# A hand-written list of 1026 operations, put in another order: linear attention and an MLP mixer on one core

## The chip, the core and the metric

The kernel runs on one core of a Trainium2 chip. The core has TensorE (PE in the profile; its weight loads are PEld), VectorE (DVE), ScalarE (ACT), GpSimd (POOL) and SyncE (SP), each with its own queue of instructions that it works off in order. DMAs are issued by SP, ACT and POOL and carried by 16 DMA engines. Matmul results land in PSUM, which the kernel cuts into eight banks of 128 x 512 fp32. The metric is the device time of one execution in microseconds; the time of a kernel is the median of its runs.

## What is computed

Inputs are q, k, v and f_logit (4 batches, 8 heads, 768 steps, 48 channels per head) and four weight matrices. Attention is a recurrence over the steps with a forget gate, and its output, as x of 768 x 384 per batch, goes through a mixer over tokens and one over channels:

```python
f = 1.0 / (1.0 + np.exp(-f_logit))
for t in range(S):
    state = f[:, :, t, :, None] * state + np.einsum('bhd,bhe->bhde', k[:, :, t], v[:, :, t])
    y[:, :, t] = np.einsum('bhd,bhde->bhe', q[:, :, t], state)
...
h = np.maximum(xt @ w_tok1, 0.0) @ w_tok2
u = x + h.transpose(0, 2, 1)
h2 = np.maximum(u @ w_ch1, 0.0) @ w_ch2
return (u + h2).astype(np.float32)
```

## The kernel before

**Attention, per batch b (0 to 3) and chunk P (0 to 2), 256 steps each.** The loads bring f, k, q and v of a chunk (POOL's DMAs, cast to bf16 for k, q, v; the first f loads go by SP and ACT). ScalarE makes the gate's logarithm: Exp and Ln at L457 and L459, or Softplus at L454 for the first two chunks. VectorE adds pairs of steps (`two`, L448; for later batches also the remainder `two_lo`, L470), PE sums them over the steps by a triangular matrix (`sums`, L479 to L482, and `totals`, L486), VectorE forms `first` (L499), ScalarE takes four exponentials (`GG`, L502 and L519) and the decay of a block (`glast`, L505, or `ends`, L509, with a small DMA on SP, L515). VectorE multiplies q and k by them (`qk`, L448, two instructions a chunk).

q and k are then transposed. Batches 0 and 1 do it on PE (L546) with a copy out of PSUM to qT and kT (L434 on ScalarE, L436 on VectorE). Batches 2 and 3 (`TURNED = 2`) do it by DMA transposes on SP (L531, "turned tiles"): kT directly, qT by way of qJ and a copy on POOL or ScalarE (L438, L434). Then come on PE the scores (L581), the parts of the state (L599), and, when VectorE (L624), or for four tiles ScalarE and POOL (L619, L621), has masked the scores to `AmT`, the outputs (L665) with the carried state (L657). VectorE carries `state` on (L633 to L641), and copies to `state_bd` follow on POOL, ACT or DVE.

**Mixer, per batch.** Outputs are copied to `x_bf` and `x_nat`; tok1 (L709, twelve matmuls), `h1T`, tok2 (L725), `u_bf`; a transpose to `uT`, on PE (L766) for batches 0 and 1 and by DMA on SP (L755, `U_TURNED`) for batches 2 and 3; ch1 (L784, 24 groups of three matmuls of 384 columns) with a ReLU to `zT` on ScalarE or VectorE (L443, L445); ch2 (L803, groups of four matmuls); the addition to `x_nat` (L814) and the store on SP (L702).

**What sets the order.** The body of the kernel issues nothing but a few memsets: `add` notes each operation with the engines that may do it, what it needs and makes, its PSUM bank and a kind for its cost. `Plan.best` then walks the constant `ORDER`. A code c stands for operation c // 4, on its engine number c % 4:

```python
for code in ORDER:
    op = self.ops[code // 4]
    e = op.engine = op.engines[code % 4]
```

For each it works out a start from what the operation needs, from its engine and its bank, takes the bank that comes free first, puts idle matmuls (`steady`, L852) into longer pauses of PE ahead of 25.5 us of its own count, and sorts by start; the operations are issued in that order. Thus the order on each engine's queue is that of `ORDER`, and the planner's times settle the banks and the number of idle matmuls. The constants `HELD` and `SLOTS` say when it takes the first loads to land, and it lets POOL hold eight loads under way.

Of the kernel before, what the change touches and what calls it, by code (L numbers as in the profile page):

```python
# [20 lines left out]
TURNED = 2  # L21
NQ = 2
ORDER = (
    0, 4, 12, 16, 24, 28, 32, 8, 20, 188, 192, 196, 36, 40, 44, 76, 68, 48, 52, 60, 208, 356, 212, 220, 64, 224,
    236, 240, 228, 360, 364, 368, 248, 244, 216, 376, 232, 372, 380, 388, 260, 80, 84, 265, 384, 200, 88, 296,
    252, 92, 96, 56, 300, 256, 72, 309, 304, 396, 392, 204, 312, 268, 272, 504, 408, 400, 276, 288, 404, 316,
    292, 280, 413, 508, 512, 320, 324, 100, 104, 108, 416, 420, 516, 448, 428, 452, 536, 532, 524, 520, 461,
    457, 544, 540, 112, 116, 120, 284, 124, 128, 132, 432, 136, 328, 332, 340, 440, 344, 464, 336, 468, 348,
    352, 444, 140, 476, 472, 556, 561, 528, 436, 424, 548, 552, 704, 592, 676, 708, 680, 564, 568, 596, 576,
    572, 584, 588, 580, 480, 484, 488, 600, 604, 608, 612, 616, 493, 497, 144, 148, 152, 501, 621, 624, 156,  # L30
    712, 684, 688, 692, 696, 716, 720, 724, 700, 728, 780, 812, 732, 736, 784, 816, 796, 800, 748, 752, 764,
    768, 820, 804, 740, 789, 756, 772, 808, 792, 852, 860, 868, 865, 856, 872, 844, 836, 828, 1188, 1192, 849,
    833, 972, 976, 824, 744, 776, 840, 1212, 1216, 980, 1036, 1012, 1028, 948, 1033, 760, 1220, 1224, 953, 1040,
    984, 1016, 996, 1020, 1001, 1025, 1004, 932, 1009, 1044, 988, 1060, 892, 1236, 1232, 1244, 1228, 1248, 1064,
    1048, 896, 1196, 1200, 1252, 1256, 993, 937, 1268, 1273, 1260, 900, 916, 1052, 876, 884, 905, 1264, 920,
    1056, 880, 888, 1368, 1372, 1276, 1280, 1284, 1288, 1292, 1240, 160, 164, 168, 172, 1376, 176, 180, 184,
    628, 1300, 1304, 1312, 1388, 1392, 1384, 1316, 1204, 1320, 1128, 908, 1132, 924, 1308, 1296, 1324, 1408,
    1380, 913, 1168, 1340, 1344, 1136, 940, 964, 1348, 1208, 1528, 1328, 1532, 1400, 1404, 928, 1336, 1356, 968,
    1352, 944, 1412, 1140, 1536, 1540, 1424, 1564, 1560, 1544, 1548, 1552, 1416, 1172, 1176, 956, 1108, 1429,
    1420, 1180, 960, 1572, 1568, 1432, 1436, 1440, 1444, 1448, 632, 636, 640, 644, 2204, 1332, 1364, 1360, 1396,  # L40
    1556, 1184, 1456, 1464, 1468, 1452, 1472, 1112, 1584, 1576, 1580, 1088, 1092, 1484, 1460, 2208, 1588, 2212,
    1480, 1476, 2216, 1592, 1596, 1600, 1604, 1096, 1612, 1608, 1500, 1504, 1488, 1620, 1624, 1616, 1496, 1492,
    1512, 1628, 1068, 1508, 1744, 1716, 1720, 1724, 1748, 1516, 1520, 1636, 1632, 1524, 2228, 2232, 2388, 1640,
    1644, 1752, 1648, 1728, 2236, 1116, 1652, 1656, 1660, 1664, 1732, 1736, 1756, 2392, 2240, 2264, 2260, 2244,
    2248, 648, 652, 656, 660, 664, 668, 672, 1668, 1120, 1760, 1741, 1764, 1769, 1072, 2396, 2272, 2268, 1808,
    1820, 1832, 1812, 1148, 1784, 1836, 2252, 2412, 2408, 1816, 1840, 1824, 1828, 2404, 1796, 1772, 1152, 1788,
    1800, 1776, 2284, 1884, 1868, 1876, 1888, 1880, 1872, 2276, 1076, 3144, 1780, 1792, 1804, 2400, 1156, 2044,
    2004, 2220, 2420, 2424, 1080, 1160, 1100, 2009, 2432, 2428, 1860, 2068, 2076, 2280, 1844, 2028, 1864, 2293,
    2072, 1996, 1848, 2001, 2012, 1852, 2036, 2224, 2048, 2016, 1856, 2552, 2288, 2020, 2025, 2556, 2040, 2080,
    2032, 1988, 1916, 1992, 2296, 2300, 2304, 2308, 2312, 1920, 3148, 1672, 2416, 1084, 2256, 2444, 2436, 1676,  # L50
    2316, 2332, 2560, 2564, 1932, 2340, 1936, 1964, 1956, 2052, 2324, 2328, 2057, 2320, 1968, 2336, 2576, 2572,
    2568, 2440, 2060, 1908, 2588, 1912, 2584, 3168, 2344, 1961, 3172, 2348, 2596, 2184, 1892, 1900, 2448, 1896,
    2064, 1904, 2188, 1680, 2452, 1684, 1688, 1692, 2456, 2460, 2464, 2468, 2472, 2476, 2592, 2144, 3176, 2148,
    2192, 2488, 2480, 2492, 2360, 2364, 2368, 2580, 2608, 2600, 3180, 2352, 2356, 2496, 1696, 1700, 2505, 2196,
    3184, 3200, 3204, 2484, 2381, 3212, 3188, 3192, 2376, 3208, 1980, 2152, 2164, 2168, 2384, 3152, 2373, 1704,
    2501, 2508, 1985, 2512, 2521, 2517, 2617, 1924, 1940, 1945, 2604, 2172, 2176, 2524, 2528, 2532, 2612, 2156,
    1708, 1712, 1928, 2540, 3156, 2548, 2544, 2536, 3160, 2620, 2624, 2628, 2632, 2636, 2648, 2652, 2640, 2644,
    2656, 2104, 2665, 2660, 3164, 3328, 3332, 1948, 2724, 2728, 2084, 3492, 1953, 2732, 2696, 2700, 2668, 2672,
    2676, 2704, 2736, 2680, 2685, 2688, 1972, 2708, 2712, 2740, 2716, 2744, 2088, 3336, 2721, 1977, 3496, 3196,
    3224, 3216, 2748, 2752, 2756, 2764, 3220, 2776, 2768, 2780, 2092, 2800, 2804, 3352, 3348, 2692, 2784, 3340,  # L60
    2808, 3344, 3360, 2761, 2773, 3232, 3228, 2788, 2812, 2108, 2124, 2112, 2816, 2096, 2792, 2821, 3368, 2796,
    3364, 3236, 3240, 3244, 3248, 3252, 3260, 2128, 3500, 2132, 2824, 2828, 3372, 3272, 3268, 3264, 2848, 2856,
    2860, 2852, 2136, 3256, 3504, 2116, 2888, 2864, 2880, 2832, 3528, 3512, 3284, 3000, 2984, 3276, 3280, 2892,
    2837, 2989, 3300, 3304, 3317, 3005, 3524, 2868, 3508, 3516, 2884, 2976, 2960, 2840, 2928, 3532, 2980, 2933,
    2944, 2968, 2936, 2949, 3016, 2844, 2964, 3536, 3288, 3384, 2973, 2941, 2872, 2920, 3380, 2896, 2952, 2957,
    2876, 3020, 3313, 2924, 2900, 2912, 2916, 2904, 2909, 3308, 3388, 3044, 3376, 1104, 3520, 1124, 3356, 3548,
    1144, 3540, 1164, 3292, 3296, 3392, 3396, 3400, 3404, 3408, 3412, 3416, 3420, 3320, 3324, 3557, 3024, 3028,
    3048, 3552, 3052, 3032, 3544, 3424, 3432, 3436, 3440, 3444, 3448, 3428, 3452, 3056, 3560, 3564, 3568, 3572,
    3636, 3456, 3460, 3580, 3584, 3588, 3592, 3576, 3036, 3596, 3064, 3008, 3013, 3068, 3640, 3464, 3468, 3472,
    2992, 3600, 3604, 3484, 3489, 3476, 3608, 3612, 3620, 3664, 3668, 3616, 3629, 3672, 3676, 3644, 3648, 3680,  # L70
    3652, 3656, 3684, 3688, 3632, 3480, 3624, 2997, 3661, 3104, 3124, 3692, 3696, 3704, 3708, 3716, 3108, 3084,
    3752, 3728, 3740, 3128, 3072, 3088, 3132, 3112, 3092, 3720, 3724, 3701, 3713, 3136, 3744, 3096, 3756, 3764,
    3732, 3116, 3760, 3748, 3737, 3768, 2180, 2160, 2100, 3040, 2200, 3120, 3812, 3796, 3816, 3801, 3860, 3820,
    3825, 3844, 3828, 3852, 3780, 3772, 3784, 3856, 3788, 3804, 3836, 3792, 3808, 3832, 3849, 3865, 3076, 3777,
    4004, 3956, 3884, 4008, 3932, 3840, 3888, 3964, 3868, 3892, 3916, 3968, 3873, 3924, 3972, 3976, 3961, 4012,
    3900, 4016, 3876, 3984, 3988, 3948, 3953, 3929, 3905, 3896, 3936, 3920, 3880, 4064, 3940, 3908, 3912, 2120,
    2140, 3080, 3980, 3140, 3060, 3100, 3944, 4024, 3992, 3996, 4044, 4048, 4052, 4028, 4032, 4056, 4068, 4036,
    4060, 4000, 4020, 4040, 4072, 4076, 4080, 4084, 4088, 4092, 4096, 4100,
)
KEPT = 3  # L80
SOFT = (0, 1)
# [804 lines left out]
```

## Time and profile before

| | |
|---|---|
| time, median of 3 runs | 166.11 us (165.85 to 166.55) |
| the profiled execution, in all | 167.62 us |
| its span | 165.9 us |
| granted TensorE clock, mean | 0.997 |
| PE busy, share of the span | 96% |
| DVE, ACT, POOL busy | 78%, 64%, 37% |
| HBM read, written | 25.17 MB, 4.72 MB |

In the rows, L803 is line 803 of the kernel; times are in us from the start of the span unless marked ns. A row of the timeline gives start, length, engine, line, operation, output and inputs, count, and in brackets how long the engine had been idle before and what ended it. A row of the stretches gives for a stretch the busy time of PE, PEld, DVE, ACT and POOL with their instruction counts, then the granted clock, the DMA engines' mean busy time in us and GB/s. A row of the chain of waits gives start, length and what the chain ran through. A row of DMA issues gives what was moved, the queue, the count, the KB of each (where shown) and the us from issue to landing. Busy times of PE are modelled, as matmuls are pipelined.

### The profile page before, as it was taken

Reading aid. Unit: us, or ns where it says so; the run is one execution under the profiler, and the core shown is the slowest. Engines: PE = TensorE matmul, PEld = TensorE weight load, DVE = VectorE, ACT = ScalarE, POOL = GpSimd, SP = SyncE. Lnnn points to the kernel's source line nnn. Section 1 sums busy time; section 2 is a strip of 40 time slices with the busy share of each in tenths; the row PEclk is TensorE's granted clock in tenths of the full one; section 3 lists DMA queues with packets and bytes.
Section 4 is the critical chain, followed back from the end, with each engine's and each line's share of the span. In section 5 each row is a group of like instructions: output and inputs, shape, how many; then the busy total and the mean of one; then the engine's idle time right before and its main releaser. Section 6 shows DMA issues by size and latency. Waiting matters only on the chain.

```text
span 165.9 us, 4990 instructions
## 1 busy us (share of the span) xinstructions
PE 158.6 (96%) x2052; PEld 101.4 (61%) x2052; DVE 128.8 (78%) x284; ACT 106.9 (64%) x231; POOL 61.7 (37%) x86
## 2 busy tenths in 40 slices
PE   7889997999999999999999999999999999999992
PEld 3356765566667766666666765665666665656661
DVE  6748997589999999998999999988599526704331
ACT  3869784797899999999948966384811511623300
POOL 7961799964776820001914514200322020000000
PEclk9999999999999999999999999999999999999998
DMA  4999999999999999457699990991900030690506
GB/s 123 219 177 171 201 210 232 168 206 227 219 225 222 225 242 142 81 98 115 133 224 128 119 155 0 106 213 50 209 19 4 0 59 16 175 325 17 177 31 206
DMA packets 68183, 24.34 MB, mean 147 GB/s; under 512 B 60896, under 2 KB 67296, under 8 KB 68160
## 3 DMA queue, kind: packets, MB, share of 16 engines
q0 software_dynamic: 41856, 13.77, 68.2%
q1 hardware_dynamic: 25776, 10.06, 28.9%
q8 instruction: 16, 0.26, 0.7%
q10 hardware_dynamic: 528, 0.20, 0.4%
q14 instruction: 7, 0.06, 0.1%
HBM read 25.17 MB, written 4.72 MB: 180 GB/s over the span
## 4 chain that ended last, share of the span: by engine, by line
PE 82%; DMA 5%; ACT 4%; DVE 4%; issue 1%; POOL 1%; DVEq 0%; ACTq 0%; POOLq 0%
PE ps L803 28%; PE ps L784 28%; DMA qk_sb<-in_q_dram 5%; PE ps L709 5%; PE ps L725 4%; PE ps L665 3%; PE ps L581 3%; PE ps L657 2%; PE ps L546 2%; PE ps L599 2%; PE ps L766 1%; PE ps L481 1%; ACT state_bd L434 1%; ACT x_nat L434 1%; DVE qk L448 1%
## 5 line engine op out<-in xcount | busy, mean ns | idle before, releaser
L803 PE MATMUL ps<-w_ch,zT 128*128 128x384 bf16 (+2 forms) x300 | 54.0, 320 | 0.0
L784 PE MATMUL ps<-uT,w_ch 128*128 128x384 bf16 x288 | 51.6, 326 | 0.0
L784 PEld LDWEIGHTS <-w_ch 128*128 128x128 bf16 x288 | 27.8, 98 | 17.6
L803 PEld LDWEIGHTS <-zT 128*128 128x128 bf16 x300 | 27.9, 98 | 17.1
L443 ACT ACTIVATE zT<-ps 128x384 bf16<-128x384 f32 x57 | 25.1, 493 | 16.3 <-PE ps L784 16.1
L624 DVE TENSOR_TENSOR AmT<-ps,mask 128x512 bf16<-128x512 f32 x44 | 28.6, 685 | 1.5 <-PE ps L581 1.2
L445 DVE TENSOR_SCALAR zT<-ps 128x384 bf16<-128x384 f32 x39 | 20.6, 553 | 10.0 <-PE ps L784 8.9
L814 DVE TENSOR_TENSOR x_nat<-x_nat,ps 128x384 f32<-128x384 f32 (+2 forms) x25 | 13.1, 534 | 10.5 <-PE ps L803 10.5
L438 POOL CAST state_bd<-state 48x192 bf16<-48x192 f32 x15 | 5.7, 377 | 28.6 <-DVE state L641 25.8
L448 DVE TENSOR_TENSOR qk<-qk_sb,GG 128x768 bf16<-128x768 bf16 x24 | 12.9, 563 | 1.3 <-DMA qk_sb<-in_q_dram 1.3
L502 ACT ACTIVATE GG<-ps 128x384 bf16<-128x384 f32 x24 | 11.2, 485 | 3.5 <-DVE first L499 2.8
L357 POOL DMA_DIRECT2D v_sb<-in_v_dram x12 | 10.7, 894 | 6.3 <-DMA w_ch<-in_moe_w_ch_dram 3.7
L434 ACT ACTIVATE x_bf<-ps 128x384 bf16<-128x384 f32 x15 | 6.9, 483 | 8.5 <-PE ps L657 8.2
L519 ACT ACTIVATE GG<-first 128x384 bf16<-128x384 f32 x24 | 11.7, 517 | 0.2
L741 DVE TENSOR_TENSOR x_nat<-x_nat,ps 128x384 f32<-128x384 f32 x21 | 10.6, 549 | 1.4 <-PE ps L725 1.2
L357 POOL DMA_DIRECT2D qk_sb<-in_k_dram x12 | 10.9, 905 | 1.6 <-POOLq L870 0.8
L434 ACT ACTIVATE u_bf<-x_nat 128x384 bf16<-128x384 f32 x12 | 5.8, 518 | 8.6 <-DVE x_nat L741 8.6
L357 POOL DMA_DIRECT2D qk_sb<-in_q_dram x12 | 10.8, 898 | 0.5 <-DMA qk_sb<-in_q_dram 0.3
L852 PE MATMUL ps<-steady 128*128 128x512 f32 (+1 forms) x20 | 9.8, 610 | 1.0 <-DVE steady L372 1.0
L438 POOL COPY qT<-qJ 128x1024 bf16<-128x1024 bf16 x3 | 3.4, 1149 | 18.8 <-ACT zT L443 18.7
L709 PE MATMUL ps<-x_bf,w_tok 128*128 128x384 bf16 x48 | 10.4, 327 | 0.0
L434 ACT ACTIVATE x_nat<-ps 128x384 f32<-128x384 f32 x20 | 9.3, 492 | 0.1
(87 smaller groups left out, 231.3 us busy)
## 6 DMA issues: line engine op xcount, KB each, us to landing
out_dram<-x_nat SPq DMA_DIRECT2D x23, 192.0 KB, 2.3
f_sb<-in_f_logit_dram POOLq DMA_DIRECT2D x9, 384.0 KB, 8.9
qk_sb<-in_k_dram POOLq DMA_DIRECT2D x12, 192.0 KB, 8.8
qk_sb<-in_q_dram POOLq DMA_DIRECT2D x12, 192.0 KB, 9.0
v_sb<-in_v_dram POOLq DMA_DIRECT2D x12, 192.0 KB, 8.9
w_ch<-in_moe_w_ch_dram POOLq DMA_DIRECT2D x2, 576.0 KB, 9.0
w_ch<-in_moe_w_ch_dram POOLq DMA_DIRECT2D x1, 1152.0 KB, 10.6
f_sb<-in_f_logit_dram SPq DMA_DIRECT2D x2, 384.0 KB, 5.8
```

The source lines that it names most:

```text
L357: lambda eng=eng, into=held(dst[i], P), of=runs(src, b, P): eng.dma_start(out=into, in_=of),
L434: nc.scalar.activation(out_, in_, AF.Copy, bias=0.0, scale=1.0)
L443: nc.scalar.activation(out_, in_, AF.Relu, bias=0.0, scale=1.0)
L445: nc.vector.tensor_scalar(out_, in_, 0.0, None, ALU.max)
L448: (nc.vector if op.engine == DVE else nc.gpsimd).tensor_tensor(out_, a, b_, what)
L502: add(ACT, r, lambda n=n: nc.scalar.activation(GG[i][:, 1, n], sview(), AF.Exp, bias=0.0, scale=2.0 * n - 1.0), need=["tables"] if b == 0 ...
L519: add(ACT, r, lambda n=n: nc.scalar.activation(GG[i][:, 0, n], first[i], AF.Exp, bias=0.0, scale=2.0 * n - 1.0), need=[("first", i)] + ([" ...
L624: add(DVE, r, lambda into=into, made=made, m4=m4: nc.vector.tensor_tensor(into, made(), m4, ALU.mult), need=masks, make=[("AmT", i, js, pa ...
L709: add(PE, rank("tok1", rt), lambda rt=rt, kt=kt, pm=pm: nc.tensor.matmul(banks[pm.at][:, 0:DM], lhsT=w_tok1[:, kt, rt * 128:(rt + 1) * 128 ...
L784: nc.tensor.matmul(banks[pm.at][:, 0:384], lhsT=w[:, kt, c0:c0 + 128], rhs=uT[:, th, :, kt, :], start=(kt == 0), stop=(kt == 2))
L803: nc.tensor.matmul(banks[pm.at][:, 0:n1 - n0], lhsT=zT[:, kt, tt * 128:(tt + 1) * 128], rhs=w_ch2[:, kt, n0:n1], start=(kt == 0), stop=(kt ...
L814: add(DVE, rank("ch2", tt), lambda un=un, pm=pm, n=n1 - n0: nc.vector.tensor_tensor(un, un, banks[pm.at][:, 0:n], ALU.add), make=[("x_nat" ...
```

## The change

Only the constant `ORDER` is another list; its first line and its last two show the form:

```diff
 ORDER = (
-    0, 4, 12, 16, 24, 28, 32, 8, 20, 188, 192, 196, 36, 40, 44, 76, 68, 48, 52, 60, 208, 356, 212, 220, 64, 224,
...
-    2140, 3080, 3980, 3140, 3060, 3100, 3944, 4024, 3992, 3996, 4044, 4048, 4052, 4028, 4032, 4056, 4068, 4036,
-    4060, 4000, 4020, 4040, 4072, 4076, 4080, 4084, 4088, 4092, 4096, 4100,
+    0, 4, 12, 16, 24, 28, 32, 8, 20, 188, 192, 196, 36, 40, 44, 48, 56, 76, 52, 208, 60, 356, 216, 212, 220,
...
+    2100, 3120, 4060, 4020, 4040, 4000, 3980, 4072, 4076, 4084, 4088, 4092, 4096, 4080, 4100,
 )
```

The new list holds the same 1026 operations. Decoded by the rule above, 90 of them are given to another engine: ScalarE has 234 in place of 232, VectorE 266 in place of 268, POOL, SP and PE as many as before (84, 53 and 389). What moved, as far as it is spoken of below:

- Batch 0, VectorE: `first` of chunk 1 (code 368) stands behind the first `qk` product of chunk 0 (code 244) instead of ahead of both; kT of chunk 0 is copied by ScalarE (code 257 in place of 256) and qT by VectorE; three mask products of chunk 0 follow `two` of chunk 2 directly, ahead of chunk 1's kT, instead of two.
- Batch 0, PE: `totals` of chunk 0 ahead of its sums; the state's parts ahead of the transposes for chunk 0 and ahead of the scores for chunk 1; fewer tok1 matmuls between the chunks.
- Batch 0, POOL: the load of w_ch1's first half (128) ahead of POOL's first mask product; its second half and f, k and q of batch 1 ahead of the next two mask products.
- POOL later: the loads of f, k, q and v of batch 3 chunk 1 and of f of chunk 2 (1684, 1688, 1692, 1696, 1700) ahead of the copy of qT of batch 2 chunk 1 (2452) instead of behind it; two more qT copies change between POOL and ScalarE.
- Batch 2 chunk 0: the second `qk` product (2272) behind the addition after tok2 group 0 of batch 1 (1776), so its turned tiles (2284 and the next) are later on SP; its scores stand behind three more groups of ch1.
- Mixer: the order of ch1 and ch2 groups within a batch, the engine of 57 ReLU, copy and other operations, and the place of the stores of batches 0 to 2 on SP. The last five PE groups are the same (ch2 of batch 3, the last row group, in its two pieces); the row group before it is number 0 instead of 3.

## What is predicted

> **What bounds the kernel now.** I read the page's busy times first, then the one wait of TensorE (PE) that matters later, then the stretches, then the chain that ended last.
>
> ```profile
> span 165.9 us, 4990 instructions
> PE 158.6 (96%) x2052; PEld 101.4 (61%) x2052; DVE 128.8 (78%) x284; ACT 106.9 (64%) x231; POOL 61.7 (37%) x86
> ```
> ```profile
> PE ps L665 <- issue: 1.0, 1, 1.0
> ```
> ```profile
> 25.00:30.00 5.00, 4.01 (x99) 2.67 (x92) 3.38 (x6) 2.39 (x6) 4.62 (x6) 1.00 1.39 218
> 50.00:55.00 5.00, 5.00 (x52) 3.27 (x54) 5.00 (x10) 4.94 (x14) 3.38 (x4) 1.00 1.83 213
> 70.00:75.00 5.00, 5.00 (x43) 3.32 (x41) 5.00 (x13) 5.00 (x10) 0.00 (x0) 1.00 0.58 102
> ```
> ```profile
> 2.34 8.39 DMA qk_sb<-in_q_dram
> ...
> 10.85 1.04 DVE qk L448 x2
> ...
> 26.53 0.99 issue
> ...
> 34.12 2.93 PE ps L784 x18
> ...
> 162.27 0.69 DVE x_nat L814 x2
> ```
>
> The reader is to see three stages. Up to about 34 us the chain runs through a load (q of the first chunk lands at 2.34 + 8.39 = 10.73), VectorE, ScalarE, and once through a stop of 0.99 us in which PE waits for nothing that the profile shows. From there to 162 us PE is busy all the time (5.00 of 5.00, granted clock 1.00), with VectorE and ScalarE nearly as full. Then come an addition and the last store. So a new order can gain only before 34 us, or at the end, which it leaves as it is (the last five groups of matmuls and the last stores are the same). From 34 to 162 us the same matmuls can only be kept from waiting, as they are now, or made to wait.
>
> **The change, part by part.** The 1026 operations are the same, 90 of them on another engine; nothing is added or removed but idle matmuls of the start, whose count follows the order. I follow what moved.
>
> *The start.* The rows of before, for chunks 0, 1 and 2 of batch 0:
>
> ```profile
> 8.97 0.56 DVE L499 TENSOR_TENSOR first<-ps,f_sb 128x384 f32<-128x384 f32 x1 [0.96 <-PE ps L486]
> 12.37 1.02 ACT L434 ACTIVATE qT<-ps 128x1024 bf16<-128x1024 bf16 x1 [1.39 <-PE ps L546]
> 13.28 0.69 DVE L436 COPY kT<-ps 128x1024 bf16<-128x1024 bf16 x1
> 14.93 0.83 ACT L459 ACTIVATE f_sb<-f_sb 128x768 f32<-128x768 f32 x1
> 15.33 0.64 PE L581 MATMUL ps<-qT,kT 48*64 48x128 bf16 x28
> 15.86 0.56 DVE L448 TENSOR_TENSOR two<-f_sb 128x384 f32<-128x384 f32 x1 [0.19 <-issue]
> 18.43 0.64 PE L581 MATMUL ps<-qT,kT 48*64 48x128 bf16 x32
> 20.65 0.86 ACT L502 ACTIVATE GG<-ps 128x384 bf16<-128x384 f32 x2
> 22.28 1.28 DVE L624 TENSOR_TENSOR AmT<-ps,mask 128x512 bf16<-128x512 f32 x2
> 24.46 0.64 PE L581 MATMUL ps<-qT,kT 48*64 48x128 bf16 x32
> 25.69 1.14 POOL L621 TENSOR_TENSOR AmT<-AmT,mask 128x512 bf16<-128x512 bf16 x1 [0.38 <-ACT AmT L619]
> 27.52 0.18 PE L665 MATMUL ps<-v_sb,AmT 64*128 64x48 bf16 x1 [0.99 <-issue]
> 28.07 0.58 PE L665 MATMUL ps<-v_sb,AmT 64*128 64x48 bf16 x32
> 28.76 1.55 PE L709 MATMUL ps<-x_bf,w_tok 128*128 128x384 bf16 x8
> ```
>
> Chunk 0: VectorE's `first` of chunk 1 ran at 8.97; now it stands behind the first `qk` product, which waits for the load until 10.85, so it ends at 10.85 + 0.5 + 0.55 = 11.9. ScalarE has chunk 1's four exponentials behind it (0.43 each, from pairs of 0.86) and the small `glast` (0.2): until 13.8. Then a state copy (0.3), an exponential of f (0.83) and the copy of kT, now ScalarE's (1.02, by qT's row): 15.8. Chunk 0's scores start at 15.85, 0.5 later.
> Chunk 1: the logarithm of f (0.83) follows, so `two` of chunk 2 starts at 16.65 (15.86 before), and on VectorE three mask products (0.62 apart) and kT (0.69) stand behind it: 17.15 + 1.85 + 0.65 = 19.65 for the scores, 1.2 later than 18.43.
> Chunk 2: here the delay is covered. Before, 6 us lay between the two scores, in which ScalarE also made copies that now come later or on VectorE. With the same durations `first` ends at 20.1, the last exponential at 21.75, the `qk` products at 22.4, qT at 24.2, kT at 24.45: scores at 24.5, as before (24.46).
> After that the new order is shorter. Chunk 1's two mask products on POOL run at 22.3 to 24.5, so its outputs follow chunk 2's scores at once (25.1 to 25.9). Chunk 2's POOL product (1.14) ends at 27.0 and its outputs run from 27.1 instead of 28.07; the eight tok1 matmuls follow at about 28.0 instead of 28.76: **-0.75**. This holds if PE's 0.99 stop does not come back. It sat in chunk 1's outputs after some 350 matmuls, and the list has nearly the same matmuls ahead of that place. If it comes back behind 25.9, all behind it moves by 0.65 (part of it is waiting anyway): **-0.1**. Both ends are kept; nothing says which, so I take the middle, **-0.4**.
>
> POOL's issues in the start: the first half of w_ch1 goes ahead of the first mask product, and the second half with f, k and q of batch 1 ahead of the next two.
>
> ```profile
> 26.79 0.94 POOL L357 DMA_DIRECT2D qk_sb<-in_q_dram  x1
> ```
>
> At 0.9 us each the last four run from 18.4 to 22 (q left at 26.79 before), and ScalarE delivers chunk 1's part at 22.2: POOL is free in time. Without that cover each issue late would move chunk 1's outputs by 0.9.
>
> *POOL in the middle, and the turned tiles.*
>
> ```profile
> 49.88 0.89 POOL L357 DMA_DIRECT2D f_sb<-in_f_logit_dram  x1 [0.53 <-DVE zT L445]
> ...
> 58.42 0.87 POOL L357 DMA_DIRECT2D v_sb<-in_v_dram  x1 [0.50 <-DMA v_sb<-in_v_dram]
> 78.00 1.15 POOL L438 COPY qT<-qJ 128x1024 bf16<-128x1024 bf16 x1 [18.71 <-ACT zT L443]
> 79.09 0.89 POOL L357 DMA_DIRECT2D f_sb<-in_f_logit_dram  x1
> ```
> ```profile
> 54.97 0.58 PE ps L581 x31
> ...
> 68.44 0.97 PE ps L725 x6
> ...
> 77.73 0.57 PE ps L581 x32
> ...
> 107.38 3.90 PE ps L784 x24
> ```
> ```profile
> 67.50 1.36 SPq L531 DMA_TRANSPOSE qJ<-qk  x1
> 102.74 3.84 SPq L755 DMA_TRANSPOSE uT<-u_bf  x2
> ```
> ```profile
> f_sb<-in_f_logit_dram POOLq DMA_DIRECT2D x9, 384.0 KB, 8.9
> ```
> ```profile
> kT<-qk SPq DMA_TRANSPOSE x1, 3.9
> ```
> ```profile
> kT<-qk SPq DMA_TRANSPOSE x1, 6.8
> ```
>
> Five loads (f, k, q, v of batch 3 chunk 1, f of chunk 2) stood behind POOL's copy of qT and left at 79.09. Now they stand ahead of it. The eight issues from 49.88 to 58.42 were 1.2 apart, so these leave from 59.6 to 64.5; with 8.9 us to landing the last is in near 73.4. That clears 79 to 83 us, where no turned tile hurt PE anyway.
> It meets batch 2 chunk 0. There the second `qk` product now waits for VectorE's addition behind tok2 group 0, which PE reaches 1.8 us later in the new list (three L784 groups of 0.49, and a few small ones, are ahead of it); that group ended at 69.4 in the row at 68.44. So 71.2 + 0.55 + 0.55 = 72.3; qJ is issued then (67.50 before), kT 1.36 later at 73.7. kT lands at 77.6 if it takes 3.9 as before, at 80.5 with the 6.8 that the tile at 92.6 took beside loads. The scores moved too, behind three more L784 groups: 77.73 + 1.46 = 79.2. The wait is 0 to **1.3**. The loads are just over by then, so I take **+0.2**.
> The Trainium skill (DMA: Bandwidth & Descriptors, section on queues, rings and completion order) says that each DMA engine takes turns between queues packet by packet, so that a transfer beside loads is slowed to a share and not queued behind the whole backlog. The rows 3.9 and 6.8 agree; by the rule alone, a doubling of 3.9 would end at 81.5, a wait of 2.3.
>
> *Other moved waits.*
>
> ```profile
> 53.25 0.68 DVE L436 COPY kT<-ps 128x1024 bf16<-128x1024 bf16 x1
> ```
>
> Batch 2's uT is turned after a tok2 that comes one ch2 group of four matmuls (0.65) later: issued at 103.4, 3.2 to land, needed at 107.38; cost 0, and the slack that goes is 0.65 of 1.4. Batch 1 chunk 1's scores come 0.5 earlier against the same VectorE work; kT's copy ended at 53.25 + 0.68 = 53.93 and the scores began at 54.97, so 0.5 of slack stays: 0, and 0.5 at most if VectorE is late. Stores go later on SP, where nothing waits for them before batch 3 rewrites x_nat: 0.
>
> **Sum**, against the profiled execution's own span: 165.9 - 0.4 + 0.2 = 165.7. The execution took 167.62 in all, 1.7 around the span, while the timed median is 166.11; I move the median by the same -0.2: **165.9**.
>
> **The rivals.**
> 1. *The start gains in full.* The 0.99 stop falls where PE waits anyway, and turned tiles stay at 3.9: -0.75 to -1, 165.2. For it: the stop is one event, and the 25 to 30 us stretch holds 0.99 of idle PE. Against it: nearly the same matmuls precede.
> 2. *Turned tiles late (slower).* kT of batch 2 chunk 0 takes 6.8 us beside the advanced loads: a wait of 1.3 of PE at its scores, and with the start as forecast 166.11 - 0.4 + 1.3 = 167.0. The wait begins when kT takes over 5.5 us, and outweighs the start's 0.4 from 5.9 on. Against it: the loads should end at 73.4, before kT is issued.
> 3. *The stop grows.* Loads of the start now leave earlier, q of batch 1 by some 5 us, into a stretch in which the DMA engines were busy 1.39 of 5 us against 1.83 later. If the stop is a fetch and grows by half of what the turned tile grew, 1.45: -0.75 + 0.99 + 1.45 = +1.7, 167.8. Nothing shows yet that it is a fetch.
> 4. *The list does not do what it says*: VectorE falls behind in 50 to 75 us, where it is at 5.00 of 5.00, and each late copy stops PE by its 0.5 or so; two or three such waits give 167.2.
>
> **How the numbers follow.** About 0.5%, 0.83 us, is what a measurement here can tell from no change. Forecast, the start's gain mostly given back, 165.3 to 166.9: 0.40. Rival 1: 0.25. Rival 2: 0.13; rival 3: 0.12; rival 4: 0.10. So faster 0.25, same 0.40, slower 0.35. The range goes from 165.0 (rival 1 with a little more) to 167.9 (rival 3's price), and leaves out some 0.17; the forecast's own is 165.3 to 166.9.
>
> **What would show it.** Right: scores of chunk 0 near 15.9, of chunk 1 near 19.6, of chunk 2 near 24.5, tok1's last eight near 28 to 28.7, the first L784 at 33.2 to 33.9; PE at 5.00 in every stretch from 35 to 160; kT of batch 2 chunk 0 landing before 79. Wrong: a wait of PE on `qT`, `kT` or `uT` behind 60 us, an issue stop of over 1.5 us, or chunk 2's scores behind 25.5, since then the cover I claimed is not there.

## The result, and the profile after

The changed kernel takes **167.89 us** (median of 4 runs, 167.84 to 169.7), the kernel before 166.11 (165.85 to 166.55, 4 runs): a ratio of 1.0127, 95% interval 1.0086 to 1.0168. Forecast was 165.9. The profiled execution of the changed kernel took 167.93 in all, its span is 166.2.

What TensorE (PE) waited for, from the waits view of the changed kernel (us in total, times, longest):

```profile
PE ps L852 <- issue: 1.1, 1, 1.1
...
PE ps L581 <- ACT kT L434: 0.3, 1, 0.3
PE ps L725 <- ACT h1T L443: 0.3, 1, 0.3
PE ps L803 <- ACT ends L509: 0.2, 1, 0.2
```

Four of its stretches:

```profile
25.00:30.00 5.00, 3.89 (x92) 2.83 (x90) 2.41 (x5) 2.56 (x7) 4.88 (x7) 1.00 1.54 225
50.00:55.00 5.00, 5.00 (x132) 3.66 (x123) 5.00 (x10) 5.00 (x14) 4.14 (x6) 1.00 1.78 228
70.00:75.00 5.00, 5.00 (x43) 3.35 (x41) 4.50 (x12) 5.00 (x13) 0.00 (x0) 1.00 0.45 101
90.00:95.00 5.00, 4.81 (x73) 3.06 (x72) 4.95 (x12) 4.60 (x11) 3.56 (x6) 1.00 1.09 113
```

And its start on PE, from the timeline:

```profile
14.57 0.64 PE L581 MATMUL ps<-qT,kT 48*64 48x128 bf16 x32 [0.35 <-ACT kT L434]
...
18.38 0.64 PE L581 MATMUL ps<-qT,kT 48*64 48x128 bf16 x32
...
24.17 0.64 PE L581 MATMUL ps<-qT,kT 48*64 48x128 bf16 x32
...
25.02 0.57 PE L665 MATMUL ps<-v_sb,AmT 64*128 64x48 bf16 x32
26.70 0.38 PE L852 MATMUL ps<-steady 128*128 128x512 bf16 x1 [1.11 <-issue]
...
28.00 0.58 PE L665 MATMUL ps<-v_sb,AmT 64*128 64x48 bf16 x32
...
28.69 1.46 PE L709 MATMUL ps<-x_bf,w_tok 128*128 128x384 bf16 x8
...
33.90 3.09 PE L784 MATMUL ps<-uT,w_ch 128*128 128x384 bf16 x18
```

The middle is full again, but for 0.19 in 90 to 95; the stop with no cause shown has come back, with 1.11 us. Yet against the profile of before there is almost nothing to explain: the span has grown by 0.3, and ch1 (line 784) starts at 33.90 against 33.96 (the timeline's first start; the chain has it 0.16 later in both). The medians differ by 1.8. So the first question is not the change but **the execution that stood for the kernel before**: its 167.62 lies 1.5 above its own median, while 167.93 is an ordinary time of the changed kernel.

### The profile page after: what moved, and what is told of

Same layout as the page of the kernel before. It is cut to its first block, busy times and chain, and to the rows that moved or that the text cites. A ratio compares the mean times of both kernels' runs of the same rounds, so it can differ in the third digit from the quotient of the medians.

```text
span 166.2 us, 4998 instructions
## 1 busy us (share of the span) xinstructions
PE 159.5 (96%) x2057; PEld 102.1 (61%) x2057; DVE 126.7 (76%) x282; ACT 109.0 (66%) x233; POOL 63.3 (38%) x86
## 3 DMA queue, kind: packets, MB, share of 16 engines
HBM read 25.17 MB, written 4.72 MB: 180 GB/s over the span
## 4 chain that ended last, share of the span: by engine, by line
PE 83%; ACT 6%; DVE 5%; issue 3%; POOL 1%; POOLq 0%; DVEq 0%
PE ps L784 28%; PE ps L803 28%; PE ps L709 5%; PE ps L725 4%; PE ps L581 4%; PE ps L665 3%; PE ps L657 2%; PE ps L546 2%; PE ps L599 2%; ACT GG L502 2%; PE ps L486 1%; POOL qk_sb L357 1%; PE ps L481 1%; PE ps L766 1%; DVE first L499 1%
## 5 line engine op out<-in xcount | busy, mean ns | idle before, releaser
L803 PE MATMUL ps<-w_ch,zT 128*128 128x384 bf16 (+2 forms) x300 | 52.6, 320 | 0.2 <-ACT ends L509 0.2
L443 ACT ACTIVATE zT<-ps 128x384 bf16<-128x384 f32 x60 | 27.6, 493 | 14.1 <-PE ps L784 11.5
L624 DVE TENSOR_TENSOR AmT<-ps,mask 128x512 bf16<-128x512 f32 x44 | 28.7, 682 | 1.2 <-PE ps L581 1.0
L445 DVE TENSOR_SCALAR zT<-ps 128x384 bf16<-128x384 f32 x36 | 18.7, 551 | 7.5 <-PE ps L784 7.3
L438 POOL COPY qT<-qJ 128x1024 bf16<-128x1024 bf16 x5 | 5.7, 1148 | 22.2 <-ACT GG L502 17.8
L852 PE MATMUL ps<-steady 128*128 128x512 f32 (+1 forms) x25 | 12.1, 595 | 2.1 <-issue 1.1
L519 ACT ACTIVATE GG<-first 128x384 bf16<-128x384 f32 x24 | 12.2, 530 | 2.3 <-DVE first L499 2.3
L434 ACT ACTIVATE x_bf<-ps 128x384 bf16<-128x384 f32 x17 | 7.9, 488 | 5.0 <-PE ps L657 3.0
L434 ACT ACTIVATE u_bf<-x_nat 128x384 bf16<-128x384 f32 x13 | 6.5, 542 | 6.2 <-DVE x_nat L741 4.1
L725 PE MATMUL ps<-h1T,w_tok 128*128 128x384 bf16 x48 | 9.4, 326 | 0.3 <-ACT h1T L443 0.3
```

Source lines behind the costliest of these rows:

```text
L434: nc.scalar.activation(out_, in_, AF.Copy, bias=0.0, scale=1.0)
L443: nc.scalar.activation(out_, in_, AF.Relu, bias=0.0, scale=1.0)
L445: nc.vector.tensor_scalar(out_, in_, 0.0, None, ALU.max)
L624: add(DVE, r, lambda into=into, made=made, m4=m4: nc.vector.tensor_tensor(into, made(), m4, ALU.mult), need=masks, make=[("AmT", i, js, pa ...
L725: nc.tensor.matmul(banks[pm.at][:, 0:DM], lhsT=w_tok2[:, kt, tt * 128:(tt + 1) * 128], rhs=h1T[:, kt, :], start=(kt == 0 and not held), st ...
L803: nc.tensor.matmul(banks[pm.at][:, 0:n1 - n0], lhsT=zT[:, kt, tt * 128:(tt + 1) * 128], rhs=w_ch2[:, kt, n0:n1], start=(kt == 0), stop=(kt ...
```

## Experiments

Line numbers of kernels with more lines are shifted: by 3 in h_newstart and h_oldstart, by 1 where the small matmuls come in. All times are medians with 1 to 5 rounds; ratios are to the kernel before in the same job.

**1. Both kernels again, and each start with the other's rest.** The two mixed lists take one list's codes up to the first line-784 matmul of batch 0's mixer (the expectations call it batch 1 chunk 1), and then the other list's codes that are left:

```diff
-ORDER = before                    # or: after
+ORDER = after[:cut] + [c for c in before if c // 4 not in taken]
```

> The kernel before, again, with a profile of its own. Theory A: the profiled execution from which I priced the change (span 165.9, 167.62 in all) was a slow one for this kernel. A typical one has a span near 164.3 (166.1 less the 1.7 around it), with the first q/k product on VectorE at about 9.4 us instead of 10.85, or without the 0.99 us stop of TensorE near 26.5 us, or both; its first matmul of batch 1 chunk 1 (line 784) then starts at about 32.5 instead of 34.1. Rival B: a typical execution starts like the one profiled (line 784 first at 34.1) and the 1.5 us come from behind it, or from what lies around the span: then the span is 165.5 to 166 again, or the gap is under 1 us.

> The changed kernel, again. Both theories: 167.8 to 167.9, span near 166.1, line 784 first at 34.1, a stop of TensorE of about 1.1 us in front of the tok1 matmuls near 25.6 us. If the stop is a matter of chance, as the 0.99 of before would be under theory A, one of its executions shows it gone.

> The new list and the new engines up to the first matmul of batch 1 chunk 1, and the list of before from there on. Theory A (the loss lies in the start, because the start of before is typically 1.5 us shorter than in the execution I read): as slow as the changed kernel or nearly, 167.2 to 167.9. Theory C (the loss lies behind 34 us: loads ahead of the turned tiles, VectorE behind, banks of the state): 166.1, as before.

> The list and the engines of before up to the first matmul of batch 1 chunk 1, and the new list from there on. Theory A: 166.1 to 166.6 (the new list lost 0.47 us behind 34 us in the profiles read so far). Theory C: 167.5 to 167.9.

Measured: before 166.24 (165.57 to 167.97, 8 runs; the profiled execution 166.11, span 164.4); after 167.87 (167.83 to 168.05), ratio 1.0117 (1.0102 to 1.0132); new start with old rest 167.46 (167.44 to 167.51), 1.0091 (1.0076 to 1.0106); old start with new rest 166.22, 1.0008 (0.9991 to 1.0024). The timeline of the kernel before in this ordinary execution:

```profile
14.45 0.64 PE L581 MATMUL ps<-qT,kT 48*64 48x128 bf16 x28
...
17.56 0.64 PE L581 MATMUL ps<-qT,kT 48*64 48x128 bf16 x32
...
23.57 0.64 PE L581 MATMUL ps<-qT,kT 48*64 48x128 bf16 x32
24.14 0.82 PE L852 MATMUL ps<-steady 128*128 128x512 bf16 x3
...
25.07 0.57 PE L665 MATMUL ps<-v_sb,AmT 64*128 64x48 bf16 x31
25.98 0.18 PE L665 MATMUL ps<-v_sb,AmT 64*128 64x48 bf16 x1 [0.35 <-issue]
...
27.23 1.55 PE L709 MATMUL ps<-x_bf,w_tok 128*128 128x384 bf16 x8
...
32.42 3.09 PE L784 MATMUL ps<-uT,w_ch 128*128 128x384 bf16 x18
```

Theory A holds. In an ordinary execution of the kernel before, VectorE does not wait for the q load; its first q/k product starts at 9.71, not 10.85:

```profile
9.71 1.01 DVE L448 TENSOR_TENSOR qk<-qk_sb,GG 128x768 bf16<-128x768 bf16 x2
```

And the stop is 0.35, not 0.99: line 784 starts at 32.42, and the new list loses 33.81 - 32.42 = **1.39 us in the start** (its second profile has 33.81). From line 784 to the end of the span the new rest takes 132.3 (166.1 - 33.81, and 164.5 - 32.19 behind the old start), the old one 132.0 (164.4 - 32.42, 165.7 - 33.73): the other 0.3.

**2. What the stop is.** The profile has two queues of instructions among its DMA queues; one of them carries 16 packets with 0.26 MB, 16 KB each. In 23.7 to 24.8 us of the kernel before it moved one of them:

```profile
q8 instruction: 1, 0.02, 5.5%
```

And this is what PE and PEld had done when the stop began, by the counts in the stretches from 0 into the stop (before, then after):

```profile
0.00:25.90 25.90, 23.98 (x349) 15.48 (x350) 20.53 (x60) 19.04 (x37) 18.89 (x27) 1.00 1.42 184
```
```profile
0.00:26.50 26.50, 24.21 (x350) 15.21 (x351) 20.75 (x60) 19.43 (x37) 20.09 (x28) 1.00 1.41 186
```

The same 700 instructions or so, in lists that do different work there. (These views leave out PE's semaphore instructions. With them, as the trace records them, the stop stands behind exactly 705 instructions in eight of the traces, those of both kernels among them; in five more behind 701 to 704, and those traces lack one to four rows in all.) Hence the theory tested from here on: PE has run out of instructions. With 16 blocks for some 4,120 PE rows, a block is about 256 instructions; experiments 3 and 4 give the number exactly. Two things were tried on it, the work in front of the stop and GpSimd's loads beside it:

```diff
 e2_noidle (of the kernel before)
-            if e == PE and free[PE] < until and t - free[PE] > 270:
+            if e == PE and free[PE] < 22300 and t - free[PE] > 270:
 e2_tok_back (of the kernel before; codes of tok1: 704, 676, 708, 680)
-    552, 704, 592, 676, 708, 680, 564, ... 480, 484, 488, 600
+    552, 592, 564, ... 480, 484, 704, 676, 488, 680, 708, 600
 e2_loads_early (of before): GpSimd's 124, 128 ahead of 284; 132, 136, 140, 144 ahead of 432; 148 behind 444
 e2_loads_late (of after): 124, 128, 132 behind 284; 136 behind 432; 140 behind x_bf; 144, 148 behind 580
```

In the last three the idle matmuls are written out as a table, where the planner had put them in the list they come from.

> The kernel before without its three idle matmuls behind chunk 2's scores (0.66 us in all); nothing else differs. Theory S (TensorE runs out of instructions behind its 349th matmul, and goes on when the next 16 KB of them have landed, whatever it did meanwhile): TensorE gets there 0.66 earlier and stands still for 0.35 + 0.66 = 1.0 us; the line 784 matmuls start as before (32.4 to 32.6), and the time stays at 166.1 to 166.2. Rival F (the stop has a size of its own, a fetch that starts when the instructions are used up): a stop of 0.35 again and 0.66 less, 165.5.

> The kernel before with the four tok1 matmuls of chunk 0's rows (0.166 us each) taken from ahead of chunk 2's scores and put behind chunk 1's outputs, where the new list has them; the idle matmuls are held where they are before. If work ahead of the stop is free because TensorE would wait there anyway, and work behind it costs its whole duration: 4 x 0.166 = 0.66 later, 166.8. If the order of these four does not matter: 166.1.

> The kernel before with GpSimd's loads of the start (w_ch1, then f, k, q, v of batch 1) in the places of the new list, ahead of its mask products; the other engines are as before. Theory L (these loads are what makes TensorE's instructions land 0.6 us later in the new list): the stop ends near 26.6 instead of 26.0 and the time is 166.6 to 166.8. Rival O (the order of TensorE's own work up to the stop does it): the stop ends at 26.0, 166.1 to 166.2; GpSimd's issues (0.9 each) in front of chunk 1's mask products are then free.

> The changed kernel with those loads of GpSimd back in the places of before; idle matmuls held as in the changed kernel. Theory L: the stop ends near 26.0 instead of 26.6 and the time falls by 0.6 to 167.2 to 167.3. Rival O: 167.8 to 167.9, with the stop's end at 26.5 to 26.6.

*The loads.* Early in the old list they cost nothing (166.23, 1.0014, 1.0000 to 1.0028): theory L is out. Late in the new list they made it slower, 169.07 (1.0191, 1.0156 to 1.0227), for a reason neither theory had: POOL's copy to x_bf now stands behind their issues, and tok1 waits for it.

```profile
27.04 0.49 PE L709 MATMUL ps<-x_bf,w_tok 128*128 128x384 bf16 x2 [1.28 <-ACT state_bd L434]
...
29.88 1.30 PE L709 MATMUL ps<-x_bf,w_tok 128*128 128x384 bf16 x7 [0.90 <-POOL x_bf L438]
```

The first row is the stop again, behind 698 matmuls and weight loads against 701 (this trace has four rows fewer in all). It is put down to a state copy that ended at 26.64, 0.40 before, which shows how such a name is to be read.

*The idle matmuls.* Without them PE waited 0.55 for a copy of ScalarE in the same place, so it came to the stop no earlier and the test of its size failed; the stop ended at 25.98 as before. The profiled execution took 166.03 and has line 784 at 32.21. The median, 167.43 with runs from 165.77 to 169.46, comes from executions that left no profile: two of them had a mean granted clock of 0.99, the rest is not explained.

*tok1* cost nothing where 0.66 was expected (166.06, 1.0008, 0.9986 to 1.0030). The profiled execution lay 1 us above that median; a second one is ordinary:

> The kernel before with the four tok1 matmuls of chunk 0's rows behind chunk 1's outputs, a second time, to have the profile of an ordinary execution (the first one profiled was 1 us above its median). It took no more than the kernel before (166.06). If the edge of the block decides (350 matmuls and 351 weight loads, then the stop), moving four matmuls of 0.166 also moves the edge by four pairs: two tok1 matmuls and two of chunk 2's outputs are done ahead of the stop, only two tok1 stand behind it, and line 784 starts within 0.15 of 32.6. If it is something else that hides them, the stop lies elsewhere or is gone.

```profile
24.81 0.57 PE L665 MATMUL ps<-v_sb,AmT 64*128 64x48 bf16 x32
25.31 0.50 PE L709 MATMUL ps<-x_bf,w_tok 128*128 128x384 bf16 x2
25.65 0.47 PE L657 MATMUL ps<-state_bd,qT 128*128 128x96 bf16 x4
25.96 0.49 PE L709 MATMUL ps<-x_bf,w_tok 128*128 128x384 bf16 x2
...
32.37 3.09 PE L784 MATMUL ps<-uT,w_ch 128*128 128x384 bf16 x18
```

166.06 again. The four instruction pairs taken from ahead of the count let four others in, and two of the tok1 matmuls are done before the block arrives at about 25.8 (the instruction behind the first 705 starts at 25.86): line 784 at 32.37, as expected within 0.15 of before. What stands ahead of the block edge and what behind is a matter of counting.

**3. Moving the count.** If blocks are asked for by count, more instructions in a place where PE waits anyway should bring the next ones earlier. One idle matmul of 0.86 us near 13 us is replaced by very small ones, a weight load and a matmul each:

```diff
-        for one in [steady32] * (n // 4) + [steady] * (n % 4):
+        for one in [steady32] * (n % 100 // 4) + [steady] * (n % 4) + [None] * (n // 100):
+            one, rows, cols, width = (one, 128, 128, 512) if one is not None else (steady, 64, 64, 16)
```

> The kernel before, with one idle matmul of 0.86 us in front of chunk 0's state products (near 13 us, where TensorE waits) replaced by 32 very small ones, that is 32 more pairs of weight load and matmul. Theory C (TensorE's instructions come in blocks of 256; the block behind the stop is asked for 5.9 us after the one before it, and that one when TensorE has passed about its 320th instruction, in chunk 1's scores): the count is reached about 2 us earlier, both blocks come earlier, and the stop of 0.35 is gone; line 784 starts 0.2 to 0.4 earlier, time 165.7 to 165.9. Rival (the stop hangs on the time, or on the loads in flight): 166.1 with the stop as before, or later by the small matmuls' own time.

> The changed kernel with one idle matmul of 0.86 us near 12.4 us replaced by 16 very small ones. Theory C: 32 more instructions are passed ahead of chunk 1's scores, the two blocks are asked for about 0.7 us earlier, and the stop's end moves from 26.6 to about 25.9; 16 more small matmuls of the outputs fall behind it (0.27): 0.4 to 0.45 less, 167.4 to 167.5. Rival: 167.8 to 167.9.

> The same with 32 very small ones. Theory C: the blocks are asked for over 2 us earlier, the stop near 25.6 is gone, and what is left in its place is the wait for ACT or POOL, if there is one: 0.8 to 1.0 less, 166.9 to 167.1. Rival: 167.8 to 167.9.

> The changed kernel without the one idle matmul behind the stop, in front of the first tok1 matmul. If all that stands behind the stop costs its whole duration: 0.22 less, 167.65. If TensorE would wait there for something else (x_bf): 167.8 to 167.9.

With 32 of them the changed kernel takes **166.82** (1.0064, 1.0040 to 1.0088), 1.05 less than 167.87, and the stop is gone:

```profile
25.02 0.70 PE L665 MATMUL ps<-v_sb,AmT 64*128 64x48 bf16 x32
25.65 0.39 PE L853 MATMUL ps<-steady 128*128 128x512 bf16 x1
25.88 0.49 PE L709 MATMUL ps<-x_bf,w_tok 128*128 128x384 bf16 x2
...
32.86 3.09 PE L784 MATMUL ps<-uT,w_ch 128*128 128x384 bf16 x18
```

With 16 it took 167.89 (167.36 to 168.16) where 167.4 to 167.5 was expected; only the lowest of its four runs is there. The profiled one had chunk 0's scores 0.6 late. Its stop of 0.57 lies 14 matmuls earlier in the program, and again at the same count:

```profile
0.00:26.50 26.50, 24.36 (x350) 15.49 (x351) 20.11 (x59) 18.73 (x35) 19.46 (x28) 1.00 1.42 188
```

Dropping the single idle matmul behind the stop gave 167.63, 0.24 less than 167.87 as expected (0.22): what stands behind the edge is paid in full.

In the kernel before, the same cure gained 0.27 at line 784 (32.15) and nothing in the time: 166.13. The chain of waits shows where it went, and the stretch from 0 the count:

```profile
58.72 0.28 PE ps L665 x13
58.99 0.30 issue
59.30 0.41 PE ps L665 x19
```
```profile
0.00:59.20 59.20, 56.83 (x861) 37.22 (x862) 50.98 (x121) 48.62 (x101) 42.79 (x54) 1.00 1.57 205
```

861 + 862 is 1022 more than 350 + 351. With the semaphore instructions the stop stands behind 1729, and 1729 - 705 is 1024: four blocks of 256. The 64 small instructions in place of the idle matmul's four (the trace has two weight loads and two matmuls for it) had moved a later edge into a run of small matmuls.

**4. Controls, and a version for both.**

```diff
 the table of idle matmuls, operation: units (4 = one of 0.86 us, 100 = one small one)
-{..., 78: 6, ..., 176: 1}      after
+{..., 78: 2, ..., 176: 1}      e4_less_idle_after
+{..., 78: 3202, ...}           e4_tiny32_drop1_after
-{..., 78: 8, ...}              before, and the old start with the new rest
+{..., 78: 1204, ...}           e4_tiny12_before
+{..., 78: 3204, ...}           e4_oldstart_tiny32, e5_best
```

> The changed kernel with the same idle matmul of 0.86 us near 12.4 us taken away and nothing put in its place: the control for the 32 small ones. Theory C (blocks of 256 instructions, counted): two instructions fewer are counted, the stop stays, 167.8 to 167.9. Rival I (what helped was the idle matmul's going, not the count): 166.8 to 167.2.

> The changed kernel with the 32 small matmuls and without the idle one behind chunk 1's outputs. If both gains are work taken off TensorE's path behind 25 us they add: 167.87 - 1.05 - 0.24 = 166.6. If the four tok1 matmuls there then wait for x_bf: 166.8.

> The kernel before with 12 small matmuls (22 more instructions counted) instead of 32. With 32 the stop near 25.6 was gone and line 784 started at 32.15 instead of 32.59, but the block edge four blocks on, at the 1729th instruction, fell into chunk outputs at 59.0 us and cost 0.30. Theory C: with 22 that edge falls behind those outputs, no stop there, and the blocks of the start still come 0.5 to 0.6 earlier: 165.7 to 165.9. Rival (the 0.30 at 59 us is not an edge of a block, or the start does not set the end): 166.1.

> The list of before up to the first matmul of batch 1 chunk 1 and the new list behind it, with the 32 small matmuls in the start. Theory C: line 784 starts at 32.1 to 32.2; the new list from there took 132.1 to 132.2 (131.8 for the old one), in it 0.19 at line 803; the 1729th instruction falls elsewhere than in the old list, near 58.6, with its block there at 58.4 to 58.8: 165.9 to 166.2.

> The start of the list of before with the 32 small matmuls, and the new list behind it, a second time and in more rounds, since one look could not tell it from the kernel before (166.0 against 166.2). If its line 784 starts 0.5 to 0.7 earlier in ordinary executions and 0.35 is lost behind it: 165.9 to 166.0 again, 0.1 to 0.2 under the kernel before; otherwise no difference.

The control: without the idle matmul and with nothing in its place 167.68 (167.43 to 168.09), 0.2 less, with PE idle for 0.59 up to 26.69:

```profile
26.69 0.32 PE L709 MATMUL ps<-x_bf,w_tok 128*128 128x384 bf16 x1 [0.59 <-DVE AmT L624]
```

The view names a mask product of VectorE. With the 32 small ones VectorE's products run at the same time (from 24.70 for 1.89, here from 24.69 for 1.89) and the same matmul starts at 26.04; so this is the stop, four instructions later in the program, as four fewer stand ahead. By the medians of the two jobs, 167.68 and 166.82, some 0.86 of the 1.05 belong to the count. Small matmuls and the dropped one together gave 166.81, not 166.6: PE then waits 0.19 for x_bf, the second case named. The old start with small matmuls and the new rest has line 784 at 31.88 and takes 165.96, the second time 32.22 and 166.16: ratios 0.9984 (0.9960 to 1.0009) and 0.9997 (0.9975 to 1.0018). **No version was found that beats the kernel before.**

Twelve small matmuls in the kernel before gave 166.89 (165.97 to 168.22), a miss, in two ways. PE stood still one block earlier, at 20.39:

```profile
18.73 0.73 PE L665 MATMUL ps<-v_sb,AmT 64*128 64x48 bf16 x25
20.39 0.25 PE L665 MATMUL ps<-v_sb,AmT 64*128 64x48 bf16 x7 [0.92 <-issue]
```
```profile
0.00:20.30 20.30, 17.68 (x222) 11.42 (x223) 14.96 (x50) 14.71 (x27) 14.01 (x22) 1.00 1.49 178
```

With its semaphore instructions PE had 449 behind it, 256 fewer than 705. The first block started at 18.00 in this execution, 2.9 behind the 256th instruction, and PE went on 2.39 later. Then the granted clock fell:

```profile
20.00:25.00 5.00, 4.28 (x63) 2.93 (x63) 2.92 (x7) 3.39 (x8) 2.95 (x5) 0.66 1.16 210
```

The twelve executions part cleanly by their mean granted clock: six at 1.00 took 165.97 to 166.61, six at 0.99 took 167.18 to 168.22.

**What the blocks show.** Starts of the first two packets on the instruction queue, beside the starts of the PE instructions that stand behind the first 256 and the first 705 (in the order of the trace, semaphore instructions counted), all in us:

| kernel | behind 256 | first block | second block | behind 705 | line 784 |
|---|---|---|---|---|---|
| before, profile of the prediction | 16.64 | 19.05 | 25.06 | 27.52 | 33.96 |
| before, ordinary | 15.76 | 17.90 | 23.78 | 25.98 | 32.42 |
| before, loads early | 15.37 | 17.66 | 23.76 | 26.20 | 32.53 |
| after | 15.77 | 18.43 | 24.41 | 26.70 | 33.90 |
| after, loads late | 15.93 | 18.58 | 24.55 | 27.20 | 35.08 |
| after, 32 small | 14.71 | 16.68 | 22.94 | 25.17 | 32.86 |
| old start, new rest, 32 small | 14.39 | 16.71 | 22.58 | 24.96 | 31.88 |

The first block starts 2.0 to 2.7 behind the 256 instructions, the second 5.9 to 6.3 behind the first, and PE starts what stands behind the 705 no sooner than 2.2 behind the second. The twelve small ones, with 2.9 for the first, stand outside this; why is open.

## Why the prediction was wrong

The forecast moved the median of 166.11 by -0.2; the change was +1.8. Of the 2.0 between them 1.5 is the base and 0.5 is the sum.

- **The base** is the step that failed: "The execution took 167.62 in all, 1.7 around the span, while the timed median is 166.11; I move the median by the same -0.2." The 1.5 between the two was seen and not asked after. It lay in the start, where the change's terms were: the ordinary execution has the 256th instruction 0.88 earlier and a stop 0.64 shorter, and line 784 1.54 earlier. A start with that much slack in it showed a new order as neutral that costs 1.39: the start's term of -0.4 measures -0.06 against the execution it was priced on (33.90 against 33.96), and +1.39 against an ordinary one.
- **Chunk 0 and 1**: the order of events was right. Chunk 1's scores come 3.81 behind chunk 0's (forecast 3.8; 3.11 before). Chunk 0's own delay was 0.12, not 0.5: the 0.5 hung on the late q load. (Its chain 13.8 + 0.3 + 0.83 + 1.02 adds up to 15.95, not 15.8; nothing hangs on the 0.15.)
- **"Chunk 2: here the delay is covered"** failed too. I followed qT and kT, and not the copies of the state among them. In both lists chunk 2's state parts (line 599) stand ahead of its scores on PE and wait for such a copy. They start at 22.61 in an ordinary execution of the kernel before, and at 23.45 in the new list, where ScalarE makes one copy between the exponentials and VectorE two ahead of kT:

```profile
22.61 0.43 PE L599 MATMUL ps<-v_sb,qk 64*64 64x48 bf16 x16 [0.28 <-ACT state_bd L434]
```
```profile
19.71 0.33 ACT state_bd L434
...
23.03 0.37 DVE state_bd L436
23.41 0.04 issue
23.45 0.43 PE ps L599 x16
23.88 0.32 PE ps L852
24.20 0.61 PE ps L581 x32
```

  Scores 5.79 behind chunk 1's, not 4.85, and 0.60 later than in the ordinary execution of before. kT, which VectorE copies behind those two (23.43, 0.69 long), is ready at 24.12, so both paths end within 0.1 of the scores' start; another order of the copies was not tried.
- **The stop**: "the list has nearly the same matmuls ahead of that place" was right to the instruction, by count, and the middle of -0.4 was mis-sized. In the new list the edge is reached at 25.5 and the block arrives at 26.61 or 26.70 (25.98 before): 0.63 later. Behind it stand the four tok1 matmuls and an idle one, which before were done ahead of it or not there: 33.81 - 26.61 = 7.20 against 32.42 - 25.98 = 6.44, another 0.76. Together 1.39. Why the first block starts 0.5 later there at the same 256th instruction (15.76 and 15.77) stays open; the places of GpSimd's loads do not do it.

The Trainium skill (Runtime: NRT & Kernel Launch, section on instruction fetch mechanics) says that instructions are refilled in blocks of 16 KiB, 256 instructions, and that a crossing is mostly hidden. The size agrees with the 256 and 1024 instructions between stops and the 16 packets of 0.26 MB; that it is hidden does not hold here, where PE stood still for 0.30 to 1.11 at edges in runs of small matmuls.

- **The middle**: qJ issued at 72.24 and kT at 73.63 (forecast 72.3 and 73.7), the scores at 78.93 (79.2):

```profile
72.24 1.34 SPq L531 DMA_TRANSPOSE qJ<-qk  x1
...
73.63 4.19 SPq L531 DMA_TRANSPOSE kT<-qk  x2
```

  The wait there is nil instead of +0.2: rival 2 did not come. What came is a wait on `ends` at 94 us, 0.19, on the path of the new rest's 0.3; that it is the cause of it was not tried, and 0.1 of the 0.3 was not traced.
- **Rival 3** named 167.8, and the stop did grow, from 0.35 to 1.11, with a block that came 0.6 later at the same count; the loads that rival 3 blamed are excluded by the two runs that moved them. That 167.8 is close to the measured 167.89 is luck: its sum stands on the untypical start too. The cost zero of POOL's early issues was right. Of the signs named to show the steps right, line 784 at 33.2 to 33.9 (33.90) and tok1's last eight at 28 to 28.7 (28.69) came true though the forecast was wrong: they were drawn from the same untypical start.

## What to carry to other kernels

Compare the profiled execution with the median before any term is priced on it; a gap larger than the effect sought is to be placed first. In stretches of many small matmuls count PE's instructions as well as its time: an idle matmul behind a block's edge cost its whole length here, and an insertion that heals one edge moves all later ones. That long matmuls are better placed ahead of an edge is not shown: moving four of them behind it cost the kernel before nothing, as the count let four other pairs in.

## What the runs showed of the hardware

- PE's instructions arrive in blocks of 256; at an edge in a run of small matmuls PE can stand still for 0.2 to 1.1 us, and the profile names no cause or a wrong one. Most of the 16 edges passed without one.
- Of the kernel before, the same program, 25 executions in one job lay between 165.59 and 169.3, mostly within 165.6 to 166.5; seven of eight of the changed kernel lay between 167.83 and 168.05, the eighth at 169.7. What decides when the first loads land was not tried.
- Whether idle matmuls hold the clock is not shown. With 0.86 us of them replaced by twelve small ones, half of the executions lost 1 us and more, and the profiled one had a granted clock of 0.66 in 20 to 25 us, behind a stop of 0.92 at a block's edge. But the same 0.86 us replaced by 32 small ones in the kernel before, or left out of the changed kernel, kept every execution at 0.997 or more; so the stop is as good a candidate. With three taken out near 24 us two of ten were at 0.99 (169.04 and 169.46); four of the eight at 1.00 took 167.16 to 168.04 all the same, and that is not explained.
